# Stage 2 of a spectral kernel: one native fp32 product against three products of rounded high and low parts

## Chip, core and metric

The kernel runs on one core of a Trainium2 chip. The metric is device time in microseconds for one execution of the whole program; the time before is the median of three runs. The core has five engines that run side by side, each with its own queue that it works off in order: TensorE (matmuls; the profile lists its weight loads apart, as PEld), VectorE (DVE), ScalarE (ACT), GpSimd (POOL), and SyncE (SP), which here issues all DMAs.

## What is computed

The reference has two halves. The first filters every sequence in the frequency domain, the second is a gated feed-forward network with a convolution of three taps.

```python
X = np.fft.rfft(x, axis=1)                     # x: 8 x 3136 x 256
Yr = Xr @ w_r - Xi @ w_i + b_r
Yi = Xr @ w_i + Xi @ w_r + b_i
Y  = sign(Y) * max(|Y| - 0.01, 0)              # on Yr and Yi
y  = np.fft.irfft(Yr + 1j * Yi, n=3136, axis=1)
h  = max(y @ w_in, 0)                          # 256 -> 1024
c  = conv_w[0]*h[s-1] + conv_w[1]*h[s] + conv_w[2]*h[s+1]
out = (h * sigmoid(c)) @ w_out                 # 1024 -> 256
```

All inputs and the output are fp32, apart from the weights of the second half, which come as 64-bit numbers.

## The kernel before

The transform of length 3136 = 56 x 56 is done as two stages of products with tables. Stage 1 (`quads`, line 269) transforms over one factor and stores its result to a scratch tensor `sc1` in memory. Stage 2 (line 312) reads it back as `a2`, four values of u (a group, `UG` = 4) at a time, and multiplies with the table `t2`. The mix (line 340) applies the weights `w_r` and `w_i`. `shrink` (lines 352 to 354) cuts by 0.01. Stage 3 (line 363) is the first half of the inverse transform and stores to `sc2`. All this is the spectral part: eight batches of seven groups, 56 items, one item in each iteration of a loop of 60, of which stage 3 lags four iterations behind stage 2. Behind it comes the second half, with stage 4 (line 495), the products with `w_in` (line 520) and with `w_out` (line 548).

Two kinds of product are used. A native product takes fp32 operands as they are. A rounded product takes operands of the type fp32r, which holds fewer bits of the fraction; where these products are used (the mix, lines 520 and 548), each operand is split into a high part, the rounded value, and a low part, the rest, and three products (high x high, high x low, low x high) are summed in PSUM. Stages 1, 2, 3 and 4 use native products.

Inside the loop the order of the work is written out by hand (`manual_schedule`), and each engine's queue follows it. In iteration `it` it is:

1. SyncE loads `a2` of item it+2 (line 302, three buffers), in the first seven iterations the part of the table `inv1`, in the first six the part of the table `t2` that the next iteration needs (line 173), and x for stage 1 (line 261, three buffers).
2. TensorE does stage 3 of item it-4 and stage 1 of an item some eleven ahead. ScalarE and VectorE move their results out of PSUM (lines 369, 284, 285), and SyncE stores them.
3. From the fourth iteration on, VectorE does three steps of preparing the weights of the second half.
4. TensorE does stage 2 of item it: two tiles of 128 channels, four products each, 112 rows of `a2` as the stationary operand and 128 columns of `t2` as the moving one. For each tile ScalarE copies the imaginary half to `d` (line 315) and casts the result to the high part `fh` (line 316), and VectorE makes the difference `d` and the low part `fl` (lines 317 and 318).
5. `shrink` of item it-2: ScalarE makes `r` and `q`, GpSimd subtracts them.
6. `third` of item it: ScalarE casts `d` to a high part (line 323), GpSimd makes the low part (line 324).
7. The mix of item it-1: 36 rounded products of 256 columns, into three PSUM tiles. VectorE adds the bias into `p1` (line 344) and the sums into `v` (line 346).
8. In one of the early iterations (the fifth) a second stage 1 follows.

Stage 1, stage 2 and the mix share six PSUM banks (`psx`). Before the loop stands a head: the whole of stage 1 for the first batch, two more items, the weights of the mix (`load_mix`, whose raw tiles share two buffers), the first part of `t2` and the first two `a2`.

Of the kernel before, what the change touches and what calls it, by code (L numbers as in the profile page):

```python
# [9 lines left out]
F32 = mybir.dt.float32  # L10
F32R = mybir.dt.float32r
I32 = mybir.dt.int32
AF = mybir.ActivationFunctionType
ALU = mybir.AluOpType
# [3 lines left out]
B, S, D, FF = 8, 3136, 256, 1024  # L18
R = 56
U = 28  # L20
# [4 lines left out]
UG = 4  # L25
NG = U // UG
JC = 4
P = 128
# [96 lines left out]
def spectral_ffn_kernel(ctx: ExitStack, tc: tile.TileContext, x, w_r, w_i, b_r, b_i,  # L125
                        w_in, conv_w, w_out, fwd1, fwd2, inv1, inv2, out):
    nc = tc.nc
    K1, K2 = 2 * R, 2 * SP
# [13 lines left out]
    mlam, warm = small[:, 0:1], small[:, 1:2]  # L142


    with ExitStack() as ab:
        stg = ab.enter_context(tc.tile_pool(name="stg", bufs=1))
        wbp = ab.enter_context(tc.tile_pool(name="wbp", bufs=2))
        s1p = ab.enter_context(tc.tile_pool(name="s1p", bufs=2))
        c1 = ab.enter_context(tc.tile_pool(name="c1", bufs=1))
        a2p = ab.enter_context(tc.tile_pool(name="a2p", bufs=3))  # L150
        cmx = ab.enter_context(tc.tile_pool(name="cmx", bufs=1))
        DB, XRB, SL_ENG = 1, 3, nc.gpsimd
        psx = ab.enter_context(tc.tile_pool(name="psx", bufs=6, space=PSUM))
        psa = ab.enter_context(tc.tile_pool(name="psa", bufs=1, space=PSUM))

        f1 = c1.tile([P, P], F32, name="f1")[:, 0:SP]
        t2 = c1.tile([K1, U, K2], F32, name="t2")
        bias = cmx.tile([P, 2, D], F32, name="bias")
        cmx.tile([P, 96], F32, name="pad")
        wmix_hi = cmx.tile([P, NT, 3, D], F32R, name="wmix_hi")  # L160
        wmix_lo = cmx.tile([P, NT, 3, D], F32R, name="wmix_lo")
        inv1v = inv1.rearrange("p (u c m) -> p u c m", u=U // 2, c=2)
        fwd2v = fwd2.rearrange("p (u m) -> p u m", u=U)

        def split(dst_hi, dst_lo, src):
            nc.scalar.copy(dst_hi, src)
            nc.vector.tensor_tensor(dst_lo, src, dst_hi.bitcast(F32), op=ALU.subtract)
# [2 lines left out]
            nc.sync.dma_start(f1, fwd1)  # L170

        def load_t2(g):
            nc.sync.dma_start(t2[:, g * UG:(g + 1) * UG, :], fwd2v[:, g * UG:(g + 1) * UG, :])

        def load_mix():

            raw = [stg.tile([P, NT, D], F32, name=f"wm_raw{k}", tag="raw", bufs=2) for k in range(2)]
            for k in range(2):
                nc.sync.dma_start(raw[k], (w_r, w_i)[k].rearrange("(t p) e -> p t e", p=P))
            split(wmix_hi[:, :, 0, :], wmix_lo[:, :, 0, :], raw[1])  # L180
            for k, op in ((1, ALU.subtract), (2, ALU.add)):
                w = stg.tile([P, NT, D], F32, name="wm", tag="wm")
                nc.vector.tensor_tensor(w, raw[0], raw[1], op=op)
                split(wmix_hi[:, :, k, :], wmix_lo[:, :, k, :], w)

        def load_bias():

            for k in range(2):
                nc.sync.dma_start(bias[:, k, :], (b_r, b_i)[k].partition_broadcast(P))
# [66 lines left out]
        def load_x(pool, b, jc, **kw):  # L256

            xr = pool.tile([P, JC, D], F32, name="xr", **kw)
            xv = x[b].rearrange("(n h j) d -> h n j d", h=2, j=H)
            for h in range(2):  # L260
                ld = nc.sync.dma_start(xr[SP * h:SP * h + R], xv[h, :, jc * JC:(jc + 1) * JC, :])
            return xr, ld
# [37 lines left out]
        def load_a2(b, g):  # L300
            a2 = a2p.tile([K1, UG, D], F32, name="a2")
            ld = nc.sync.dma_start(a2, sc1[b].rearrange("(u q) j d -> (q j) u d", q=4)[:, g * UG:(g + 1) * UG, :])
            return a2, ld

        def stage2(g, a2):

            fh, fl = [wkf.tile([P, NT, 3, UG, SP], F32R, name=nm) for nm in ("fh", "fl")]
            d = wkf.tile([P, NT, UG, SP], F32, name="d", bufs=DB)
            for t in range(NT):
                ps = psx.tile([P, UG, 2, SP], F32, name="ps_s2", tag="bank")  # L310
                for k in range(UG):
                    nc.tensor.matmul(ps[:, k], a2[:, k, t * P:(t + 1) * P], t2[:, g * UG + k, :],  # L312
                                     start=(k == 0), stop=(k == UG - 1), skip_group_check=True)
                psv = ps.rearrange("p k c m -> p c k m")
                nc.scalar.copy(d[:, t], psv[:, 1])
                nc.scalar.copy(fh[:, t, 0:2], psv)
                nc.vector.tensor_tensor(d[:, t], psv[:, 0], d[:, t], op=ALU.subtract)
                nc.vector.tensor_tensor(fl[:, t, 0:2], psv, fh[:, t, 0:2].bitcast(F32), op=ALU.subtract)
            return fh, fl, d
# [7 lines left out]
        def mix(xs):  # L327


            fh, fl = xs  # L330
            ps = {c: psx.tile([K2, UG // 2, D], F32, name=f"ps_mx{c}", tag="bank") for c in (2, 0, 1)}
            for c in (2, 0, 1):
                q = (1, 2, 0)[c]
                for k in range(UG // 2):
                    mm = []
                    for t in range(NT):
                        a = [f[:, t, c, 2 * k:2 * k + 2, :] for f in (fh, fl)]
                        mm += [(a[0], wmix_hi[:, t, q, :]), (a[0], wmix_lo[:, t, q, :]), (a[1], wmix_hi[:, t, q, :])]
                    for n, (lt, rh) in enumerate(mm):
                        nc.tensor.matmul(ps[c][:, k, :], lt, rh, start=(n == 0), stop=(n == len(mm) - 1))  # L340
            p1 = wk.tile([K2, 2, UG // 2, D], F32, name="p1")
            v = wk.tile([K2, 2, UG // 2, D], F32, name="v")
            for c in range(2):
                nc.vector.tensor_tensor(p1[:, c], ps[2], bias[:, c:c + 1, :].to_broadcast([K2, UG // 2, D]), op=ALU.add)
            for c in range(2):
                nc.vector.tensor_tensor(v[:, c], ps[c], p1[:, c], op=ALU.add)
            return v

        def shrink(v):
            r = wk.tile([K2, 2, UG // 2, D], F32, name="r", bufs=3)  # L350
            q = wk.tile([K2, 2, UG // 2, D], F32, name="q", bufs=1)
            nc.scalar.activation(r, v, AF.Relu, bias=mlam)
            nc.scalar.activation(q, v, AF.Relu, bias=mlam, scale=-1.0)  # L353
            nc.gpsimd.tensor_tensor(r, r, q, op=ALU.subtract)  # L354
            return r

        def stage3_pe(g, r):
# [28 lines left out]
        n_it = len(items)  # L386
        WP0, LAST = 3, n_it - 6
        a2s = {}
        p1 = NG
        load_f1()  # L390
        with tc.tile_pool(name="hx", bufs=1, reuse_waits="tile") as hx:
            xh = []
            for p in range(NG):
                xr, ld = load_x(hx, 0, p, tag=f"hx{p}")
                xh.append(xr)
            with tc.issue_after(ld.ins):
                load_t2(0)
                load_mix()
                load_bias()
                st = stage1_head(xh)  # L400
        with tc.issue_after(st.ins):
# [4 lines left out]
            for i in range(2):  # L406
                a2s[i], ld = load_a2(*items[i])
        ab.enter_context(tc.issue_after(ld.ins))
        wkf, wk, cab, io = [ab.enter_context(tc.tile_pool(name=nm, bufs=n, reuse_waits="tile"))
                            for nm, n in (("wkf", 2), ("wk", 2), ("cab", 1), ("io", 2))]  # L410
        cab.tile([P, 56], F32, name="pad")
        i1 = cab.tile([K2, U // 2, 2, SP], F32, name="i1")
        wkf.tile([P, 56], F32, name="pad", bufs=1)
        wk.tile([P, 72], F32, name="pad", bufs=1)
# [9 lines left out]
                nx += 1  # L424

        with tc.manual_schedule():
            for it in range(n_it + LAG):
                if it + 2 < n_it:
                    a2s[it + 2], _ = load_a2(*items[it + 2])
                if it < NG:  # L430
                    load_inv1(it)
                    if it + 1 < NG:
                        load_t2(it + 1)
                fetch(XRB)
                if it >= LAG:
                    g3 = items[it - LAG]
                    ps3 = stage3_pe(g3[1], ss.pop(it - LAG))
                if p1 < n_it:
                    ps1 = stage1_pe(xq.pop(0))
                if it >= LAG:  # L440
                    stage3_out(*g3, ps3)
                if WP0 <= it < n_it:
                    next(background, None)
                if p1 < n_it:
                    stage1_out(*items[p1], ps1)
                    p1 += 1
                if WP0 <= it < n_it:
                    for _ in range(2):
                        next(background, None)
                if it < n_it:  # L450
                    xs[it] = stage2(items[it][1], a2s.pop(it))
                if 0 <= it - 2 < n_it:
                    ss[it - 2] = shrink(vs.pop(it - 2))
                if it < n_it:
                    xs[it] = third(xs[it])
                if 0 <= it - 1 < n_it:
                    vs[it - 1] = mix(xs.pop(it - 1))
                if p1 < n_it and p1 < min(it + AHEAD, NG + 2 + it + it // 2):
                    fetch(1)
                    ps1 = stage1_pe(xq.pop(0))  # L460
                    stage1_out(*items[p1], ps1)
                    p1 += 1
# [6 lines left out]
    wk, hp, io, y_b = pool("cwk"), pool("chp", 3), pool("cio"), pool("y_b")  # L469
# [143 lines left out]
```

## Time and profile before

| quantity | value |
|---|---|
| median of three runs | 1730.86 us (1730.43 to 1733.43) |
| the profiled execution | 1732.64 us |
| its span, first to last instruction | 1730.9 us |
| mean granted TensorE clock | 0.986 of full speed |
| spectral part | up to about 506 us |
| bytes moved by DMA | 163.77 MB, most in the spectral part |

The span is the profiled execution's time without the 1.7 us around it. A row of grouped instructions reads: line, engine, operation, the tiles written and read, the shape, the count, then after the bar the busy time in all, the mean of one in ns, and the idle time just before them with what ended it. A row of the chain in order of time reads: start, duration, engine and line or transfer, count. A row of the timeline reads: start, duration, engine, line, operation, tiles, shape, count, and in brackets the idle time before it. PEld is TensorE's load of the stationary operand, SPq the queue of SyncE. Tile names are shown without their digits: `t` is `t2`, `a` is `a2` or `a1`, `ps_s` stands for PSUM tiles of the stages.

### The profile page before, as it was taken

Reading aid. Unit: us, or ns where it says so; the run is one execution under the profiler, and the core shown is the slowest. Engines: PE = TensorE matmul, PEld = TensorE weight load, DVE = VectorE, ACT = ScalarE, POOL = GpSimd, SP = SyncE. Lnnn points to the kernel's source line nnn. Section 1 sums busy time; section 2 is a strip of 40 time slices with the busy share of each in tenths; the row PEclk is TensorE's granted clock in tenths of the full one; section 3 lists DMA queues with packets and bytes.
Section 4 is the critical chain, followed back from the end, with each engine's and each line's share of the span. In section 5 each row is a group of like instructions: output and inputs, shape, how many; then the busy total and the mean of one; then the engine's idle time right before and its main releaser. Section 6 shows DMA issues by size and latency. Waiting matters only on the chain.

```text
span 1730.9 us, 30421 instructions
## 1 busy us (share of the span) xinstructions
PE 1685.7 (97%) x12544; PEld 1556.3 (90%) x12544; DVE 1390.2 (80%) x1722; ACT 1197.5 (69%) x1589; POOL 209.9 (12%) x116
## 2 busy tenths in 40 slices
PE   4899999999998999999999999999999999999998
PEld 1688888888987999999999999999999999999998
DVE  2488888776546888888888888888888888888887
ACT  1477777677765777777777776776777677776776
POOL 0245445444440000000000000000000000000000
PEclk7899999999999999999999999999999999999999
DMA  8988888888432110111111011111101111100001
GB/s 222 250 259 244 235 248 248 217 225 237 139 101 72 54 43 23 43 54 44 43 54 44 22 43 55 43 43 55 43 22 47 51 43 44 43 22 23 22 22 43
DMA packets 115274, 163.77 MB, mean 95 GB/s; under 512 B 10680, under 2 KB 87728, under 8 KB 115136
## 3 DMA queue, kind: packets, MB, share of 16 engines
q1 hardware_dynamic: 115136, 161.83, 31.8%
q8 instruction: 99, 1.62, 0.4%
q14 instruction: 39, 0.32, 0.1%
HBM read 84.73 MB, written 77.07 MB: 93 GB/s over the span
## 4 chain that ended last, share of the span: by engine, by line
PE 95%; DMA 2%; DVE 1%; ACT 1%; issue 1%; SPq 1%; POOL 0%; ACTq 0%; DVEq 0%
PE acc L548 32%; PE ps_h L520 32%; PE ps_mx L340 14%; PE ps_s L312 7%; PE ps_s L495 6%; PE ps_s L363 3%; PE ps_s L269 3%; DMA xr<-in_x_dram 1%; DMA wm_raw<-in_w_i_dram 0%; SPq L274 0%; DVE yl L502 0%; ACT yh L501 0%; DMA sc<-ha 0%; DVE c L529 0%; DVE c L531 0%
## 5 line engine op out<-in xcount | busy, mean ns | idle before, releaser
L548 PE MATMUL acc<-wout,gh 128*128 128x256 f32 x3136 | 571.2, 281 | 0.0
L529 DVE SCALAR_TENSOR_TENSOR c<-h,cw,c 128x896 f32<-128x896 f32 x448 | 512.8, 1148 | 69.5 <-ACT c L527 66.5
L520 PE MATMUL ps_h<-yh,win 128*128 128x450 f32 x1792 | 550.3, 368 | 3.0 <-ACT yh L501 2.0
L548 PEld LDWEIGHTS acc<-wout,gh 128*128 128x128 f32 x3136 | 493.0, 188 | 6.1 <-ACT gh L534 0.3
L548 PE MATMUL acc<-wout,gl 128*128 128x256 f32 x1568 | 437.3, 280 | 0.4 <-DVE gl L535 0.4
L520 PEld LDWEIGHTS ps_h<-yh,win 128*128 128x128 f32 x1792 | 339.5, 189 | 29.3 <-ACT yh L501 2.2
L522 ACT ACTIVATE h<-ps_h 128x900 f32<-128x900 f32 x224 | 207.1, 924 | 197.5 <-PE ps_h L520 197.0
L520 PE MATMUL ps_h<-yl,win 128*128 128x450 f32 x896 | 329.8, 368 | 0.2 <-DVE yl L502 0.2
L548 PEld LDWEIGHTS acc<-wout,gl 128*128 128x128 f32 x1568 | 293.9, 188 | 1.2 <-DVE gl L535 0.6
L531 DVE TENSOR_TENSOR c<-h,c 128x896 f32<-128x896 f32 x224 | 243.7, 1088 | 40.9 <-ACT c L530 40.1
L535 DVE TENSOR_TENSOR gl<-c,gh 128x896 fp32r<-128x896 f32 x224 | 242.8, 1089 | 41.6 <-ACT gh L534 40.6
L534 ACT CAST gh<-c 128x896 fp32r<-128x896 f32 x224 | 210.7, 941 | 85.7 <-DVE c L531 85.7
L530 ACT ACTIVATE c<-c 128x896 f32<-128x896 f32 x224 | 212.5, 949 | 20.4 <-DVE c L529 18.3
L340 PE MATMUL ps_mx<-wmix_hi,fh 128*128 128x256 f32 x672 | 193.1, 287 | 0.0
L340 PE MATMUL ps_mx<-wmix_hi,fl 128*128 128x256 f32 x672 | 188.7, 281 | 1.7 <-POOL fl L324 1.7
L340 PE MATMUL ps_mx<-wmix_lo,fh 128*128 128x256 f32 x672 | 187.9, 280 | 0.0
L520 PEld LDWEIGHTS ps_h<-yl,win 128*128 128x128 f32 x896 | 169.4, 189 | 11.6 <-DVE yl L502 0.5
L527 ACT ACTIVATE c<-h,cw 128x896 f32<-128x896 f32 x168 | 175.9, 1047 | 1.8
L354 POOL TENSOR_TENSOR r<-r,q 128x1024 f32<-128x1024 f32 x56 | 133.5, 2384 | 235.8 <-ACT q L353 235.8
L312 PEld LDWEIGHTS ps_s<-t,a 112*128 112x128 f32 x896 | 106.8, 195 | 43.3 <-issue 39.2
L340 PEld LDWEIGHTS ps_mx<-wmix_hi,fl 128*128 128x128 f32 x672 | 126.6, 188 | 2.7 <-POOL fl L324 1.9
L340 PEld LDWEIGHTS ps_mx<-wmix_hi,fh 128*128 128x128 f32 x672 | 127.0, 189 | 0.4 <-issue 0.4
(77 smaller groups left out, 1715.1 us busy)
## 6 DMA issues: line engine op xcount, KB each, us to landing
xr<-in_x_dram SPq DMA_DIRECT2D x112, 224.0 KB
a<-sc SPq DMA_DIRECT2D x56, 448.0 KB
z<-sc SPq DMA_DIRECT2D x56, 448.0 KB
out_dram<-o SPq DMA_DIRECT2D x27, 896.0 KB
sc<-z SPq DMA_DIRECT2D x104, 224.0 KB
sc<-a SPq DMA_DIRECT2D x98, 224.0 KB
sc<-ha SPq DMA_DIRECT2D x14, 224.0 KB
win_bits<-in_moe_w_in_dram SPq DMA_DIRECT2D x4, 512.0 KB
```

The lines of the kernel that those rows point to most:

```text
L312: nc.tensor.matmul(ps[:, k], a2[:, k, t * P:(t + 1) * P], t2[:, g * UG + k, :], start=(k == 0), stop=(k == UG - 1), skip_group_check=True)
L340: nc.tensor.matmul(ps[c][:, k, :], lt, rh, start=(n == 0), stop=(n == len(mm) - 1))
L354: nc.gpsimd.tensor_tensor(r, r, q, op=ALU.subtract)
L520: nc.tensor.matmul(ps[:, a, 0:CH + 2], lt, rh, start=(n == 0), stop=(n == len(mm) - 1))
L522: nc.scalar.activation(h, ps[:, :, 0:CH + 2], AF.Relu)
L527: nc.scalar.mul(c, h[:, :, 0:CH], cw[:, 0, f:f + 1])
L529: nc.vector.scalar_tensor_tensor(c, h[:, :, k:k + CH], cw[:, k, f:f + 1], c, op0=ALU.mult, op1=ALU.add)
L530: nc.scalar.activation(c, c, AF.Sigmoid)
L531: nc.vector.tensor_tensor(c, h[:, :, 1:CH + 1], c, op=ALU.mult)
L534: nc.scalar.copy(gh, c)
L535: nc.vector.tensor_tensor(gl, c, gh.bitcast(F32), op=ALU.subtract)
L548: nc.tensor.matmul(acc[m // 2][:, m % 2, :], lt[:, sl], rh[:, f, :], start=(f == 0 and n == 0 and m % 2 == 0), stop=(f == NF - 1 and n == ...
```

## The change

Stage 2's native product becomes three rounded products. The table `t2` is kept as a high part `t2h` and a low part `t2l`; each part that is loaded goes to a raw tile first (in the two buffers of `load_mix`), ScalarE casts it to `t2h`, VectorE subtracts to get `t2l`. Each `a2` is split by ScalarE (cast to `ah`) and GpSimd (subtract to `al`), an iteration before stage 2 uses it. To make room, `a2` has two buffers in place of three, `p1` is dropped (the bias sum goes to `v` and is added up in place), and `q` is dropped (the second activation writes `v` in place, and GpSimd subtracts `v`). The splits of `t2` and of `a2` for item it+1 stand in iteration it ahead of stage 2 of item it; those for item 0 stand ahead of the loop.

```diff
-        a2p = ab.enter_context(tc.tile_pool(name="a2p", bufs=3))
+        a2p = ab.enter_context(tc.tile_pool(name="a2p", bufs=2))
...
-        t2 = c1.tile([K1, U, K2], F32, name="t2")
+        c1.tile([P, 96], F32, name="pad")
+        t2h = c1.tile([K1, U, K2], F32R, name="t2h")
+        t2l = c1.tile([K1, U, K2], F32R, name="t2l")
...
         def load_t2(g):
-            nc.sync.dma_start(t2[:, g * UG:(g + 1) * UG, :], fwd2v[:, g * UG:(g + 1) * UG, :])
+            raw = stg.tile([K1, UG, K2], F32, name="t2_raw", tag="raw", bufs=2)
+            nc.sync.dma_start(raw, fwd2v[:, g * UG:(g + 1) * UG, :])
+            return raw
+
+        def split_t2(g, raw):
+            sl = slice(g * UG, (g + 1) * UG)
+            split(t2h[:, sl, :], t2l[:, sl, :], raw)
...
+        def split_a2(a2):
+            ah = ahp.tile([K1, UG, D], F32R, name="ah")
+            nc.scalar.copy(ah, a2)
+            al = ahp.tile([K1, UG, D], F32R, name="al")
+            nc.gpsimd.tensor_tensor(al, a2, ah.bitcast(F32), op=ALU.subtract)
+            return ah, al
...
                 for k in range(UG):
-                    nc.tensor.matmul(ps[:, k], a2[:, k, t * P:(t + 1) * P], t2[:, g * UG + k, :],
-                                     start=(k == 0), stop=(k == UG - 1), skip_group_check=True)
+                    for n, (q, tab) in enumerate(((0, t2h), (0, t2l), (1, t2h))):
+                        nc.tensor.matmul(ps[:, k], a2[q][:, k, t * P:(t + 1) * P], tab[:, g * UG + k, :],
+                                         start=(k == 0 and n == 0), stop=(k == UG - 1 and n == 2), skip_group_check=True)
...
-            p1 = wk.tile([K2, 2, UG // 2, D], F32, name="p1")
...
-                nc.vector.tensor_tensor(p1[:, c], ps[2], bias[:, c:c + 1, :].to_broadcast([K2, UG // 2, D]), op=ALU.add)
+                nc.vector.tensor_tensor(v[:, c], ps[2], bias[:, c:c + 1, :].to_broadcast([K2, UG // 2, D]), op=ALU.add)
...
-                nc.vector.tensor_tensor(v[:, c], ps[c], p1[:, c], op=ALU.add)
+                nc.vector.tensor_tensor(v[:, c], ps[c], v[:, c], op=ALU.add)
...
-            q = wk.tile([K2, 2, UG // 2, D], F32, name="q", bufs=1)
...
-            nc.scalar.activation(q, v, AF.Relu, bias=mlam, scale=-1.0)
-            nc.gpsimd.tensor_tensor(r, r, q, op=ALU.subtract)
+            nc.scalar.activation(v, v, AF.Relu, bias=mlam, scale=-1.0)
+            nc.gpsimd.tensor_tensor(r, r, v, op=ALU.subtract)
...
+        ahp = ab.enter_context(tc.tile_pool(name="ahp", bufs=2, reuse_waits="tile"))
...
         with tc.manual_schedule():
+            split_t2(0, traw)
+            a2s[0] = split_a2(a2s[0])
             for it in range(n_it + LAG):
                 if it + 2 < n_it:
                     a2s[it + 2], _ = load_a2(*items[it + 2])
                 if it < NG:
                     load_inv1(it)
                     if it + 1 < NG:
-                        load_t2(it + 1)
+                        traw = load_t2(it + 1)
...
+                if it + 1 < NG:
+                    split_t2(it + 1, traw)
+                if it + 1 < n_it:
+                    a2s[it + 1] = split_a2(a2s[it + 1])
                 if it < n_it:
                     xs[it] = stage2(items[it][1], a2s.pop(it))
```

More of the change, by code (lines that the diff above doesn't have):

```diff
@@ L156, in spectral_ffn_kernel @@
         f1 = c1.tile([P, P], F32, name="f1")[:, 0:SP]
-        t2 = c1.tile([K1, U, K2], F32, name="t2")
+        c1.tile([P, 96], F32, name="pad")
+        t2h = c1.tile([K1, U, K2], F32R, name="t2h")
+        t2l = c1.tile([K1, U, K2], F32R, name="t2l")
         bias = cmx.tile([P, 2, D], F32, name="bias")
-        cmx.tile([P, 96], F32, name="pad")
         wmix_hi = cmx.tile([P, NT, 3, D], F32R, name="wmix_hi")
@@ L396, in spectral_ffn_kernel @@
             with tc.issue_after(ld.ins):
-                load_t2(0)
+                traw = load_t2(0)
                 load_mix()
```

## The prediction, made before the changed kernel was run

> **What bounds the kernel now.** I read the page first (engine shares, the chain by line), then the busy times by stretch, then the chain in order of time inside one iteration.
>
> ```profile
> span 1730.9 us, 30421 instructions
> PE 1685.7 (97%) x12544; PEld 1556.3 (90%) x12544; DVE 1390.2 (80%) x1722; ACT 1197.5 (69%) x1589; POOL 209.9 (12%) x116
> PE 95%; DMA 2%; DVE 1%; ACT 1%; issue 1%; SPq 1%; POOL 0%; ACTq 0%; DVEq 0%
> ```
> ```profile
> core 0: us, PE busy (x) PEld busy (x) DVE busy (x) ACT busy (x) POOL busy (x), PEclk, DMA share, GB/s
> 100.00:430.00 330.00, 329.04 (x3086) 279.87 (x3079) 260.69 (x466) 240.04 (x376) 152.98 (x81) 1.00 0.84 241
> ```
> ```profile
> 56.70 1.98 PE ps_s L312 x16
> ...
> 92.42 1.98 PE ps_s L312 x16
> 94.41 4.21 PE ps_mx L340 x36
> 98.61 1.02 PE ps_s L363 x16
> 99.64 0.86 PE ps_s L269 x8
> 100.50 1.98 PE ps_s L312 x16
> ```
>
> The chain is TensorE for 95%. In the spectral part TensorE works 329.04 of 330 us at full clock, so what its instructions need is what the time is. The chain shows one iteration: 1.98 us of stage 2, 4.21 of mix, 1.02 of stage 3, 0.86 of stage 1, together 8.08 (92.42 to 100.50). Every us added to stage 2 is added 56 times; the FFN behind it isn't touched. The other engines have room: of 8.08 us ScalarE works 5.9 (240.04/330), VectorE 6.4, GpSimd 3.7. The DMAs are the nearest neighbour, at 0.84.
>
> **The products.** What sets the 1.98 us is the question on which everything hangs.
>
> ```profile
> L340 PE MATMUL ps_mx<-wmix_hi,fh 128*128 128x256 f32 x672 | 193.1, 287 | 0.0
> L340 PEld LDWEIGHTS ps_mx<-wmix_hi,fh 128*128 128x128 f32 x672 | 127.0, 189 | 0.4 <-issue 0.4
> L340 PEld LDWEIGHTS ps_mx<-wmix_lo,fh 128*128 128x128 f32 x672 | 126.8, 189 | 0.0
> L312 PE MATMUL ps_s<-t,a 112*128 112x128 f32 x896 | 118.0, 286 | 0.0
> L495 PE MATMUL ps_s<-i,z 112*128 112x112 f32 x896 | 109.9, 277 | 4.6 <-DVE yl L483 3.1 <-DVE yl L502 1.5
> L312 PEld LDWEIGHTS ps_s<-t,a 112*128 112x128 f32 x896 | 106.8, 195 | 43.3 <-issue 39.2 <-ACT fh L323 1.6 <-ACT fh L316 1.4
> ```
> ```profile
> 253.82 1.86 PEld L312 LDWEIGHTS ps_s<-t,a 112*128 112x128 f32 x16 [0.81 <-issue]
> ...
> 506.33 3.65 PEld L495 LDWEIGHTS ps_s<-i,z 112*128 112x128 f32 x32 [0.39 <-DVE v L346]
> ```
>
> Line 312 issues 56 x 2 x 4 = 448 native products and shows 896 matmuls and 896 loads: a native product is two pairs of load and matmul. From the last rows, less one load of 0.19 us at the end, loads follow each other every (1.86 - 0.19)/15 = 111 ns in stage 2, and every (3.65 - 0.19)/31 = 112 ns in stage 4 (line 495). Stage 4 streams 112 columns, stage 2 streams 128: if streaming set the pace, stage 4 would be an eighth quicker. It isn't, and what both share is a load of 128 columns. So the load sets the pace, at 111 ns, and a shorter stream buys nothing. The mix (line 340) has the new type and 256 columns: 4.21/36 = 117 ns for one pair. Its load record is as long as the native one (189 against 195 ns), so the new type doesn't load faster.
>
> The Trainium skill, page "TensorE: Matmul & The Clock Gate", section "LDWEIGHTS (loading the stationary operand)", has a load take its number of columns over 1.2, 107 ns here; the trace's 111 agrees. The same page, "Back-to-back issue gap", states some 81 ns for pairs with 128 columns in a long stream; by that figure 24 pairs would be 1.94 us against 1.78 now (an estimate), and the two rows above speak against it.
>
> **Stage 2 after.** 16 pairs go, 4 x 2 x 3 = 24 come: 8 more at 111 ns is **+0.89 us** an iteration, **+50 us** in 56. Were all 24 to run at the mix's 117 ns, it is 24 x 0.117 - 16 x 0.111 = +1.03, or +58. I take 50: length of stream and of load are nearer to line 312 than to line 340. The ends are kept: 50 to 58 with the load as the bound.
>
> **The split of a2** (ScalarE cast, GpSimd subtract, one iteration ahead).
>
> ```profile
> L534 ACT CAST gh<-c 128x896 fp32r<-128x896 f32 x224 | 210.7, 941 | 85.7 <-DVE c L531 85.7
> L354 POOL TENSOR_TENSOR r<-r,q 128x1024 f32<-128x1024 f32 x56 | 133.5, 2384 | 235.8 <-ACT q L353 235.8
> ```
> ```profile
> 253.10 1.01 ACT L369 COPY z<-ps_s 128x1024 f32<-128x1024 f32 x1 [1.81 <-PE ps_s L363]
> 254.01 0.59 ACT L284 COPY a<-ps_s 128x512 f32<-128x512 f32 x1
> 255.07 0.37 ACT L315 COPY d<-ps_s 128x256 f32<-128x256 f32 x1 [0.47 <-PE ps_s L312]
> ...
> 258.75 0.62 ACT L323 CAST fh<-d 128x512 fp32r<-128x512 f32 x1
> ```
> ```profile
> 253.21 1.72 POOL L324 TENSOR_TENSOR fl<-d,fh 128x512 fp32r<-128x512 f32 x1
> ```
> ```profile
> 249.71 0.49 SPq L302 DMA_DIRECT2D a<-sc  x1
> ...
> 261.78 0.32 SPq L302 DMA_DIRECT2D a<-sc  x1
> ```
>
> The cast of 1024 columns is some 1.05 us (941 ns for 896, and 0.8 more per column), the subtract 2.38. ScalarE comes to 6.9 and GpSimd to 6.1 of now 8.97 us; neither is the bound. The cast sits ahead of stage 2's evacuations on ScalarE: from 254.6 to 255.65, where the engine idled 0.47 and TensorE is now busy longer. It pushes the rest (r, q, the third cast) by about 0.9 us at most: the third cast starts 4.93 us after stage 2 now, 5.85 then, when q has ended. From there GpSimd subtracts r (2.38) and makes the third low part (up to 1.72): done at 9.95. The next mix asks for it with its third pair, at 8.97 + 2.87 + 0.25 = 12.1. These 2.1 us are the cover, so the split costs **0**; what exceeds them lengthens the iteration.
>
> What shrinks is the lead of the loads of a2. With two buffers the load for it+2 waits for GpSimd to be done with a2 of it, and has to land for a cast in it+1. Two iterations hold cast, subtract, issue and landing: 1.05 + 2.38 + 0.5 + landing. With 10.49 us for a landing (quoted below) that is 14.4, under the 17.9 of two iterations: no cost. The load at 261.78 comes only 0.1 us before stage 2 (which starts 8.07 us after the 253.82 above), the one at 249.71 4.1 before. The first kind leaves 0.1 + 8.97 + 0.8 = 9.9 us, so the cast is late by 0.6, within the cover. I take **0**; the other end is a landing of 16 us (the load of 55.03 below is that of iteration 3, whose stage 2 starts at 71.15), where the ring gives (3.93 + 16.1)/2 = 10.0 us an iteration, +1.05 in each of some 42, **+44**.
>
> The smaller edits: p1 and q vanish into v, with the same additions and activations, at **0**: v is now held until GpSimd's subtract, which with two buffers ends well before the next-but-one mix writes it.
>
> **The split of t2** is the hidden part. In iterations 0 to 5 the table part for it+1 is loaded in iteration it, and ScalarE's cast of it stands in the same iteration ahead of the cast of a2 and of stage 2's evacuations. Now the load has a whole iteration.
>
> ```profile
> 1.21 3.70 DMA xr<-in_x_dram
> ...
> 12.68 7.11 DMA wm_raw<-in_w_i_dram
> ...
> 37.86 10.49 DMA xr<-in_x_dram
> ```
> ```profile
> 36.13 0.48 SPq L302
> ...
> 71.15 1.98 PE ps_s L312 x16
> ...
> 77.33 1.02 PE ps_s L363 x16
> ```
> ```profile
> 55.03 0.33 SPq L302 DMA_DIRECT2D a<-sc  x1
> 55.41 0.49 SPq L193 DMA_DIRECT2D i<-in_inv_dram  x1
> 55.96 0.45 SPq L173 DMA_DIRECT2D t<-in_fwd_dram  x1
> ```
> ```profile
> 19.81 0.62 ACT L166 CAST wmix_hi<-wm_raw 128x512 fp32r<-128x512 f32 x1 [8.41 <-DMA wm_raw<-in_w_i_dram]
> ```
>
> In SyncE's queue the order is a2, inv1, t2, x (55.03, 55.41, 55.96). The a2 load waits for the subtract of a2 two before, that subtract for its cast, and that cast is queued on ScalarE behind the t2 cast, which waits for the t2 of one iteration earlier. A **ring** closes: t2 lands, t2 cast 0.62, a2 cast 1.05, a2 subtract 2.38, issue of a2 and inv1 some 1.1, landing of the next t2. Landings in the trace: 3.7 (first load, nothing ahead), 7.1 (wm_raw, behind the x loads), 10.5 (x, in the fullest stretch). In the ring the queue empties between rounds and t2 has some 0.6 MB ahead of it; I take 7.1. One round is 0.62 + 1.05 + 2.38 + 1.1 + 7.1 = 12.25 us.
>
> The start: the first a2 are there by 49 (issued up to 36.13, ahead of the x that lands at 48.35). Cast and subtract end at 52.8; then a2, inv1 and t2 are issued, t2(1) lands at 61, the ScalarE and GpSimd work behind it ends at 65.2, and stage 2 of iteration 1 begins, where it began at 56.70. Five rounds later, at 126.5, stage 2 of iteration 6 begins. Stage 3 first runs in iteration 4 (77.33), so the rows of 92.42 and 100.50 are stage 2 of iterations 5 and 6, and the delay is 26. Of it 6 x 0.89 = 5 is counted in stage 2: +21. Once, in iteration 4, a second stage 1 at the end of the iteration puts its store in SyncE's queue ahead of the a2 load, behind all of ScalarE's work of that iteration: +5 by the casts and activations in between (r and q 1.1 each, the evacuations 2.2, the casts), so **+26**. With 3.7 us the round is 8.85 and the term +7, with 10.5 it is 15.65 and +46. VectorE's subtract of t2 (0.7 us, six times) lies beside the ring.
>
> **Sum.** The profiled execution took 1732.64: the span of 1730.9 and 1.7 around it. 1732.6 + 50 + 26 = 1809; the median of the runs, 1730.86, is 1.8 below that execution, so **1807**.
>
> **Rivals.**
> - *Two passes.* A rounded product of 128 columns has no row here; if it ran in two passes as a native one, 24 products are 48 pairs: 32 x 0.111 = +3.55 an iteration, +199; the ring then nearly hides (26 - 21 + 5 = 10). **1940**. For it: no rounded product in the trace has under 256 columns; against: the mix's 117 ns is one pass.
> - *Loads partly saved.* Two of three products share their weights; were that load skipped, 16 loads remain, stage 2 stays 1.78 and only the ring is left, +31: **1762**. Against: lines 340 and 312 show a load for every matmul, and line 340 too has two neighbours with the same weights. By the Trainium skill's 81 ns (the section named above) the time would be some 1770.
> - *Faster.* If the stream set the pace, 128 columns would take half of the mix's 117, 58 ns: 24 x 0.058 = 1.40, -0.38 an iteration, -21. With t2 landing in 3.7 us (+7, and 2 for the shorter iterations beside it) that gives **1719**. Below a pace of some 67 ns, where 24 products save 9 us, it decides; the equal pace of stage 4's shorter streams speaks against it.
> - *The a2 ring binds.* Landings of 16 us in the steady part: 1807 + 44 = **1851**. The 0.84 share of the DMAs speaks for it, the longer iteration, which spreads the same bytes over 8.97 us, against.
>
> **How the numbers follow.** Forecast 0.70, two passes 0.08, loads saved 0.06, faster 0.04, a2 ring 0.12. The forecast's own ends are 1788 (50 and 7) and 1835 (58 and 46). The range reaches from the loads-saved case to the a2 ring's: 1762 to 1851, which leaves out two passes, faster and what lies beyond the ends. A measurement of this kernel tells 0.2% (3.5 us) from no change: faster 0.04, same 0.02, slower 0.94.
>
> **What would show it.** 1344 matmuls of stage 2 with as many loads, loads 111 to 117 ns apart, stage 2 at some 2.9 us in the chain and an iteration of 9 us with TensorE still full: the first term. In the first 130 us ScalarE idle before a cast of t2 released by the t2 DMA, six times, and iterations of 12 us there: the ring. Loads 58 to 80 ns apart, or matmul records twice as many, would overturn the first term; idle TensorE between 130 and 430 us, with ScalarE waiting for a2, would show the a2 ring.

## The result: slower, 1.0343 of the time before

The changed kernel takes 1791.12 us (median of four runs, 1789.17 to 1793.31) against 1731.89 (four runs beside it): the ratio is 1.0343, interval 1.0328 to 1.0358. That is 59 us more; the forecast was 76 more, in a range of 31 to 120.

The page of the changed kernel, and its busy times behind the start, from 130 to 430 us (same columns; of before, 100 to 430 was shown):

```profile
span 1791.5 us, 31603 instructions
PE 1745.2 (97%) x12992; PEld 1613.0 (90%) x12992; DVE 1411.5 (79%) x1729; ACT 1257.7 (70%) x1652; POOL 347.6 (19%) x172
```
```profile
130.00:430.00 300.00, 299.25 (x2794) 258.95 (x2794) 230.96 (x396) 229.47 (x341) 209.24 (x100) 1.00 0.76 215
```

TensorE is the bound as before, 299.25 of 300 us; it has 448 more pairs of load and matmul (12992 against 12544), and the DMAs, with the same bytes over more time, fell from 0.84 to 0.76. In the list by line, stage 2 has three groups of 448, one load for each matmul; the chain in order of time shows one iteration:

```profile
L327 PE MATMUL ps_s<-t2h,ah 112*128 112x128 f32 x448 | 128.6, 287 | 0.0
L327 PEld LDWEIGHTS ps_s<-t2h,ah 112*128 112x128 f32 x448 | 88.3, 197 | 43.2 <-issue 36.7 <-ACT fh L338 2.4 <-ACT t2h L167 1.6
```
```profile
125.61 1.02 PE ps_s L376 x16
...
127.50 2.82 PE ps_s L327 x24
130.32 4.26 PE ps_mx L355 x36
134.58 1.02 PE ps_s L376 x16
```

From one stage 3 (125.61) to the next (134.58) it is 8.97 us, where it was 8.08. Stage 2 went from 1.98 to 2.82; the mix, 4.21 then and 4.26 now, and the rest stand. Single loads of the timeline, first and tenth of a group of 24, are (253.91 - 252.91)/9 = 111 ns apart:

```profile
252.91 0.19 PEld L327 LDWEIGHTS ps_s<-t2h,ah 112*128 112x128 f32 x1 [0.81 <-issue]
...
253.91 0.19 PEld L327 LDWEIGHTS ps_s<-t2h,ah 112*128 112x128 f32 x1
```

**Where the 60.6 us of span are.** Iteration 7 begins its stage 3 at 125.61; before, it began at 106.69, this row of its chain:

```profile
106.69 1.02 PE ps_s L363 x16
```

So 18.9 us are lost by then and 60.6 - 18.9 = 41.7 in the 49 items that follow, 0.85 each. The first seven items lose 6 at that rate. That leaves **48 us for the pairs** (56 x 0.85) and **13 us for the start**. A steady iteration is longer by 0.89, which would make 50; the mean is lower because the kernel before loses some 2 us of its own late in the loop, where its mix takes 4.41 and that of the changed kernel 4.25.

### The profile page after: what moved, and what is told of

It reads as the page before. It is cut to its first block, busy times and chain, and to the rows that moved or that the text cites. A ratio compares the mean times of both kernels' runs of the same rounds, so it can differ in the third digit from the quotient of the medians.

```text
span 1791.5 us, 31603 instructions
## 1 busy us (share of the span) xinstructions
PE 1745.2 (97%) x12992; PEld 1613.0 (90%) x12992; DVE 1411.5 (79%) x1729; ACT 1257.7 (70%) x1652; POOL 347.6 (19%) x172
## 4 chain that ended last, share of the span: by engine, by line
PE 94%; DMA 2%; ACT 1%; DVE 1%; SPq 1%; issue 1%; POOL 0%; ACTq 0%; POOLq 0%; DVEq 0%
PE acc L568 31%; PE ps_h L540 31%; PE ps_mx L355 13%; PE ps_s L327 9%; PE ps_s L515 6%; PE ps_s L376 3%; PE ps_s L276 2%; DMA t_raw<-in_fwd_dram 1%; DMA xr<-in_x_dram 1%; DMA a<-sc 0%; SPq L281 0%; DMA sc<-ha 0%; DMA sc<-a 0%; ACT ah L314 0%; DVE c L549 0%
## 5 line engine op out<-in xcount | busy, mean ns | idle before, releaser
L316 POOL TENSOR_TENSOR al<-a,ah 112x1024 fp32r<-112x1024 f32 x56 | 137.3, 2452 | 120.6 <-ACT ah L314 61.7
L367 POOL TENSOR_TENSOR r<-r,v 128x1024 f32<-128x1024 f32 x56 | 133.2, 2379 | 96.0 <-ACT v L366 94.7
```

The lines of the kernel that those rows point to most:

```text
L316: nc.gpsimd.tensor_tensor(al, a2, ah.bitcast(F32), op=ALU.subtract)
```

## Experiments

Theory A: eight more loads in each iteration are the steady cost, whatever their matmuls stream, and the splits are free there. The start had several candidates. Each ratio is to runs of the kernel before on the same chip, beside it.

| kernel | us | ratio to before, interval | steady iteration |
|---|---|---|---|
| before | 1731.9 to 1732.6 | 1 | 8.07 |
| changed | 1791.1 | 1.0343, 1.0328 to 1.0358 | 8.97 |
| e1 native product of the high parts | 1755.0 | 1.0128, 1.0108 to 1.0148 | 8.06 to 8.11 |
| e2 short streams | 1814.6 | 1.0474, 1.0447 to 1.0501 | 8.96, some 10.5 |
| e3 operands exchanged | 1747.3 | 1.0080, 1.0056 to 1.0103 | 7.70, some 8.1 to 8.6, one 13.8 |
| e4 t2 split late | 1796.0 | 1.0361, 1.0338 to 1.0385 | 8.97 |
| e5 three a2 buffers | 1786.9 | 1.0322, 1.0294 to 1.0349 | 8.97 |
| e7 a2 subtract twice | 1871.2 | 1.0782, 1.0735 to 1.0829 | 8.97, ten of 13.2 to 17.1 |
| e8 a2 cast twice | 1801.8 | 1.0396, 1.0364 to 1.0427 | 8.97 |
| e9 x loads first | 1789.2 | 1.0333, 1.0311 to 1.0356 | 8.97 |
| e10 subtract twice, weights behind the loop | 1864.3 (one run) | | 8.97 |
| e11 e5 and e9 together | 1786.6 | 1.0311, 1.0294 to 1.0328 | 8.97 |

### The products: e1, e2, e3

e1 keeps all but the products:

```diff
-                    for n, (q, tab) in enumerate(((0, t2h), (0, t2l), (1, t2h))):
-                        nc.tensor.matmul(ps[:, k], a2[q][:, k, t * P:(t + 1) * P], tab[:, g * UG + k, :], ...)
+                    nc.tensor.matmul(ps[:, k], a2[0][:, k, t * P:(t + 1) * P].bitcast(F32), t2h[:, g * UG + k, :].bitcast(F32), ...)
```

> All of the change stays (loads, splits, buffers, v in place), but stage 2 does one native product of the high parts again, 16 pairs of load and matmul instead of 24; the low parts are made and not used. Theory A (eight more loads an iteration are the steady cost, the splits cost nothing once the loop runs, the rest of the loss lies in the first 130 us): 1742 to 1746 us, which is the time before plus a start-up term of 10 to 14, iterations of 8.07 us in the steady part. Rival (the splits, the a2 buffers or the DMA lead cost in every iteration): over 1755, iterations over 8.2 us.

The chain of e1, one iteration:

```profile
252.82 1.02 PE ps_s L375 x16
...
254.70 1.98 PE ps_s L326 x16
...
260.88 1.02 PE ps_s L375 x16
```

Stage 2 is 1.98 us again and the iteration 8.06: with ScalarE's cast, GpSimd's subtract and two a2 buffers in every iteration, the steady loop runs as before. The time, 1755, missed its 1742 to 1746: its start costs 16.5 (stage 3 of iteration 7 at 123.17 in its chain, against 106.69), more than in the changed kernel (the start section comes back to it), and iterations of 8.11 and a longer end add some 5.

e2 leaves all 24 loads and shortens 16 of the streams. The low products of the imaginary half are left out:

```diff
                     for n, (q, tab) in enumerate(((0, t2h), (0, t2l), (1, t2h))):
-                        nc.tensor.matmul(ps[:, k], a2[q][:, k, t * P:(t + 1) * P], tab[:, g * UG + k, :], ...)
+                        w = P if n == 0 else SP
+                        nc.tensor.matmul(ps[:, k].rearrange("p c m -> p (c m)")[:, 0:w], a2[q][:, k, t * P:(t + 1) * P], tab[:, g * UG + k, 0:w], ...)
```

> The second and third product of each three stream 64 columns instead of 128 (the imaginary half gets no low products); the 24 loads an iteration stay. Theory A (the load of 128 columns sets the pace): 1791 within 4 us, loads still 111 to 112 ns apart. Rival (streamed columns set the pace, 256 instead of 384 for each three products): stage 2 shorter by up to a third, 0.9 us an iteration, some 1741.

Loads of the timeline (two, eleven steps apart), then the chain, then the busy times of the steady part, all of e2:

```profile
250.00 0.19 PEld L328 LDWEIGHTS ps_s<-t2h,ah 112*128 112x128 f32 x1
...
251.23 0.19 PEld L328 LDWEIGHTS ps_s<-t2h,al 112*128 112x128 f32 x1
```
```profile
269.45 4.28 PE ps_mx L356 x36
...
275.62 2.80 PE ps_s L328 x24
278.41 5.83 PE ps_mx L356 x36
```
```profile
130.00:430.00 300.00, 300.00 (x2680) 261.77 (x2679) 218.92 (x379) 218.79 (x326) 198.13 (x97) 0.95 0.74 207
```

Loads are (251.23 - 250.00)/11 = 112 ns apart, and stage 2 takes 2.80 us with a third of the streamed columns gone, 2.82 with all of them. The stream does not set the pace; the rival falls. The time none the less missed its place by 23 us, in the slow direction: the granted clock is 0.95 here instead of 1.00. In about every fourth iteration comes a stretch at half clock; here it falls on the mix, which was not edited and takes 5.83 us instead of 4.28. These are the iterations of 10.5.

e3 exchanges the roles: the table is loaded, a2 is streamed, 256 columns at a time. The result lies transposed, so it is not the reference's.

```diff
-                for k in range(UG):
+                for kk in range(2):
+                    k = 2 * t + kk
                     for n, (q, tab) in enumerate(((0, t2h), (0, t2l), (1, t2h))):
-                        nc.tensor.matmul(ps[:, k], a2[q][:, k, t * P:(t + 1) * P], tab[:, g * UG + k, :], ...)
+                        nc.tensor.matmul(ps.rearrange("p k c m -> p (k c m)")[:, kk * D:(kk + 1) * D], tab[:, g * UG + k, :], a2[q][:, k, :], ...)
```

> Stage 2 with the operands' roles exchanged: the tables are loaded (128 columns) and a2 is streamed (256 columns), so that the same three rounded products take 12 pairs an iteration instead of 24, with as many streamed columns in all; the result lies transposed and isn't the reference's. Theory A (pace of the load, until the stream is as long as the load): 12 pairs at 117 ns are 1.4 us instead of 2.7, -1.3 an iteration, near 1720; if another engine or the DMAs bind at 7.7 us, up to 1735. Rival (streamed columns or the number of multiplications set the pace): 1791, unchanged.

```profile
390.13 1.02 PE ps_s L377 x16
...
392.01 1.61 PE ps_s L328 x12
...
397.83 1.02 PE ps_s L377 x16
```

The chain of e3: the same three products, with as many streamed columns (12 x 256 = 24 x 128), take 1.61 us instead of 2.82, and the iteration is 7.70. Half the pairs, four sevenths of the time: it is the pairs that cost. That the load is what costs in a pair is argued and not shown: no run changes the width of the load. Stage 3, with loads of 64 columns, has its pairs 64 ns apart (1.02 us for 16), which speaks for the load, but its products are also smaller (64 x 64). The whole came to 1747, above the 1720 to 1735 expected: many iterations before 330 us take 8.1 to 8.6, one near 330 us takes 13.8, those at the end 7.6, and the start costs as in e1. What stretches those iterations is not shown.

### The start: e4, e5, e9, e11

The prediction put the start down to a ring through the cast of t2. The chain of the changed kernel from 40 us on:

```profile
44.81 2.35 POOL al L316
47.17 0.32 SPq L309
...
48.54 0.42 SPq L268
...
50.79 5.04 DMA xr<-in_x_dram
...
57.93 5.31 PE ps_s L327 x24
...
65.16 5.31 PE ps_s L327 x24
70.47 6.62 PE ps_mx L355 x36
...
103.81 0.33 SPq L309
...
104.72 5.54 DMA t_raw<-in_fwd_dram
```

Read from the top, the first column the start and the second the duration: the first subtract (44.81 to 47.16) releases the a2 load of iteration 0 (line 309), behind it in SyncE's queue come the x loads (line 268) for the stage 1 that stands ahead of stage 2 on TensorE, and stage 2 begins at 57.93 instead of 51.28. Then 24 pairs take 5.31 us and 36 take 6.62, twice the 2.82 and some one and a half times the 4.26 of later: half clock by their durations. (The clock record of this execution has 1.00 there; that of e5 has 0.50 over its first 24 pairs, which take the same 5.31 us.) Last, at 103.81, the ring that was predicted: a2, inv1 and t2 issued, 5.54 for t2 to land, the cast.

e4 moves the split of t2 behind `third`:

```diff
-                if it + 1 < NG:
-                    split_t2(it + 1, traw)
                 if it + 1 < n_it:
                     a2s[it + 1] = split_a2(a2s[it + 1])
...
                     xs[it] = third(xs[it])
+                if it + 1 < NG:
+                    split_t2(it + 1, traw)
```

> The split of t2 for the next iteration is moved behind stage 2, shrink and third of the current one; everything else as changed. Ring theory of the prediction (ScalarE's wait for t2 ahead of the a2 cast holds back the a2 subtract, and with it SyncE's next loads): the start-up term of some 13 us falls to 3 to 7, 1781 to 1786. Rival (the start is held by the a2 loads waiting for their buffer, with the x loads queued behind them, and by the half clock that follows): within 3 us of 1791.

It gained nothing: 1796 is above both expectations. Some 3 us of that lie in a stretch at half clock near 360 us (below). Its chain shows why this is no clean test of the ring: `t2l` now stands directly ahead of the stage 2 that needs it, and its subtract takes 1.67 us, 0.9 on the mean in the changed kernel. The ring is opened, and another wait is put in its place:

```profile
105.91 1.67 DVE t2l L168
...
107.62 3.55 PE ps_s L327 x23
```

That the ring exists, the chain of e1 shows, where TensorE has less to do and the landings of t2 come to lie on the chain:

```profile
82.38 3.92 DMA t_raw<-in_fwd_dram
...
92.25 4.62 DMA t_raw<-in_fwd_dram
...
102.93 4.92 DMA t_raw<-in_fwd_dram
```

Between the first two lie the casts, the a2 subtract and the issues, as predicted: a round of 9.9 us (9.6 in the chain of e9). In the second the a2 load waits for a stage 1 store, 10.7. A round is longer than an iteration of 8.97 by little and than one of 8.07 by more, which fits the start of 13 us in the changed kernel and of 16.5 in e1; that it is the whole of the difference is not shown.

e5 gives a2 its third buffer back (`bufs=3`), so that the first a2 load waits for nothing. e9 keeps two buffers and moves `fetch(XRB)` ahead of `load_a2`. e11 does both.

> As changed, with three buffers for a2 again. Theory B (the start is lost because the a2 load of iteration 0 now waits for the first subtract, and SyncE's queue, with the x that stage 1 ahead of stage 2 needs, waits behind it; the late start also keeps TensorE at half clock longer): stage 2 begins at some 52 us instead of 57.9, most of the 13 us come back, 1780 to 1785. Rival (the first casts, subtracts and the t2 loads are late by themselves): within 3 us of 1791.

> As changed (two buffers for a2), with the x loads of an iteration issued ahead of its a2, inv1 and t2 loads. Theory B (x behind the waiting a2 load is what delays the start): stage 2 begins earlier by 3 to 6 us, 1783 to 1788. Rival (not the order in SyncE's queue but the a2 split itself): within 3 us of 1791, or slower where a2 and t2 now land later.

> As changed, with three a2 buffers and the x loads issued first in each iteration. Theory B for the start (SyncE's queue behind the waiting a2 load): the two remedies meet the same cause, so together little more than each alone, 1780 to 1788; what stays over the time before is the pairs' 48 to 50 us and 2 to 6 at the start. Rival (two separate causes): the gains of e5 and e9 add up, 1776 or less.

The chain of e5:

```profile
40.38 9.55 DMA xr<-in_x_dram
...
52.88 5.31 PE ps_s L327 x24
...
116.94 1.02 PE ps_s L376 x16
```

Stage 2 begins at 52.88, as expected, and stage 3 of iteration 7 at 116.94 instead of 125.61: 8.7 of the 13 us are back. The time fell by 4 only (1786.9, beside the 1780 to 1785 expected), which the intervals do not separate from the changed kernel. In the profiled executions 3 us are lost again because an idle gap near 352 us, which the changed kernel has too, is followed here by a stretch at half clock: stage 2 takes 3.88 us there, and from stage 3 to stage 3 it is 13.9 us, where the changed kernel has 10.8.

```profile
351.86 0.75 issue
352.62 1.08 PE ps_s L276 x4
353.69 3.88 PE ps_s L327 x24
```

e9 begins stage 3 of iteration 7 at 118.03, 7.6 us earlier, and has the same loss near 355 us. By its time alone, 1789.2, its rival (within 3 us of 1791) would hold; the start in the trace is what speaks for theory B. Together (e11, 1786.6; stage 3 of iteration 7 at 117.35) they give no more than e5 alone: one cause, SyncE's queue behind an a2 load that waits for the first subtract. None of these four beats the kernel before; the best is 3.1% slower.

### The cover of the a2 split: e8, e7, e10

e8 issues ScalarE's cast of a2 twice (the first added line), e7 GpSimd's subtract (the second).

```diff
 def split_a2(a2):
             nc.scalar.copy(ah, a2)
+            nc.scalar.copy(ah, a2)
...
             nc.gpsimd.tensor_tensor(al, a2, ah.bitcast(F32), op=ALU.subtract)
+            nc.gpsimd.tensor_tensor(al, a2, ah.bitcast(F32), op=ALU.subtract)
```

> As changed, with ScalarE's cast of a2 issued twice. It adds 1.0 us ahead of everything that GpSimd waits for, less than the cover of 2.1. Cover theory: steady iterations stay at 8.97 us, 1791 within 5 (a few us more in the start at most). Rival (ScalarE's queue is on the path already): +0.5 us or more an iteration, over 1815.

> As changed, with GpSimd's subtract of a2 issued twice (the second writes the same values). The profile after leaves 2.1 us between the end of the third low part and the mix pair that reads it; the second subtract takes 2.4 to 2.6. Cover theory (the a2 split is free as long as GpSimd's row of work ends within those 2.1 us): the excess of 0.3 to 0.5 us shows in an iteration of 9.3 to 9.5 us, 1805 to 1820 in all. Rival (there is more cover than that, since GpSimd is busy for 8.7 of 8.97 us only): within 4 us of 1791.

e8: steady iterations stay at 8.97, so 1.0 us more ahead of GpSimd is free there. The time, 1802, is none the less outside the 5 us expected: the 10 us lie in the start (5) and in a stretch near 365 us (4). e7 is worse than either theory: ten iterations behind the start take 13.2 to 17.1 us, which is some 70 of the 80 us lost. VectorE and GpSimd in one of them, of 16.4 us (timelines), and its chain:

```profile
245.06 0.68 DVE L292 COPY a<-ps_s 128x512 f32<-128x512 f32 x1
...
248.24 4.94 DVE L223 TENSOR_SCALAR win_r<-win_bits 128x512 int32<-128x512 int32 x1
253.10 0.41 DVE L333 TENSOR_TENSOR d<-ps_s,d 128x256 f32<-128x256 f32 x1
```
```profile
245.36 2.40 POOL L316 TENSOR_TENSOR al<-a,ah 112x1024 fp32r<-112x1024 f32 x1 [0.52 <-ACT ah L314]
247.84 2.75 POOL L317 TENSOR_TENSOR al<-a,ah 112x1024 fp32r<-112x1024 f32 x1
250.55 2.35 POOL L368 TENSOR_TENSOR r<-r,v 128x1024 f32<-128x1024 f32 x1
```
```profile
250.71 1.02 PE ps_s L377 x16
...
252.59 1.62 issue
254.21 1.79 PE ps_s L276 x4
256.00 5.31 PE ps_s L328 x24
...
267.15 1.02 PE ps_s L377 x16
```

`win_r` on VectorE, 0.7 us on the mean in the changed kernel, lasts 4.94 here: it begins while GpSimd's second subtract runs, and ends (253.18) only when the one after it, to 252.90, is done too. The copy out of PSUM ahead of it (245.06) keeps its 0.68. It is not alone: line 222, which writes `win_m` from two inputs in SBUF, takes 3.6 us on the mean in e7 and 0.89 in the changed kernel (130 to 430 us), while `fl`, which reads PSUM, takes 0.68 in both. So an operation of VectorE that works on SBUF alone can stand still while GpSimd works, here through two of its instructions. The Trainium skill, "SBUF — State Buffer", section "SBUF: two separate sides", has the two engines share a pair of ports as an exclusive lock for whole instructions; of VectorE's operations it names those in a mode with two ports and those with two inputs in SBUF, and the loser waits. The trace agrees for line 222, 3.6 us against 0.89; whether `win_r`, with one input, falls under the first kind, no run shows. Behind `win_r` wait stage 2's differences, behind them PSUM banks, TensorE idles 1.62 us, and the next 24 pairs run at half clock (granted clock 0.50): 5.31 us instead of 2.82. With the stage 1 and the mix beside them, also slowed, a gap of 1.6 us costs this iteration 7.5.

e10 takes that preparation out of the loop, with the subtract still doubled:

```diff
-                if WP0 <= it < n_it:
-                    next(background, None)
...
-                if WP0 <= it < n_it:
-                    for _ in range(2):
-                        next(background, None)
...
+            for _ in background:
+                pass
```

> GpSimd's subtract of a2 twice, as in e7, and VectorE's preparation of the FFN weights taken out of the loop and done behind it, so that VectorE has hardly an operation left in the loop that reads and writes SBUF only (the whole time grows by the preparation behind the loop, some 60 to 90 us; the periods inside the loop are what is compared). Theory C (in e7 the two engines block each other on SBUF, VectorE's preparation waiting for whole GpSimd instructions, and TensorE's clock falls in the gaps that follow): iterations of 8.97 to 9.4 us between 130 and 430 us, no half clock there. Rival (GpSimd's chain is simply too long, by the excess over the cover of 2.1 us): iterations of 9.4 us and more, many of them 12 us as in e7.

```profile
130.00:430.00 300.00, 300.00 (x2810) 260.59 (x2810) 175.83 (x304) 228.98 (x337) 281.36 (x136) 1.00 0.68 208
```
```profile
251.20 1.02 PE ps_s L377 x16
...
260.17 1.02 PE ps_s L377 x16
```

The busy times and the chain of e10: GpSimd works 281 of 300 us, TensorE all 300 at full clock, an iteration is 8.97. The long iterations of e7 (16.4 us, not the 12 that this expectation gives them) come from the two engines blocking each other, not from the length of GpSimd's chain. The time of e10, from a single run, has the preparation as work of its own behind the loop and is not compared.

## Why the prediction was right, and where it was not

- **The pace of a pair** carried it. It was read from two native stages with streams of 128 and 112 columns and the same spacing, and said to hold for the rounded type. Spacing 111 ns, 24 pairs in 2.82 us (2.9 forecast), iteration 8.97 (8.97 forecast), 48 us in all (50 forecast). e2 shows the independence from the stream, e3 the dependence on the number of pairs; that the load is what sets it stays an argument. The rivals with two passes, with a saved load and with the stream as the bound are out: 448 loads for 448 matmuls in each group, one record for each product.
- **The start** was the mis-sized term: +26 forecast, 13 measured. Its entry came out right by luck (stage 2 of iteration 1 at 65.2 forecast, 65.16 measured). The forecast let the first subtract end at 52.8 and t2 land at 61; the subtract ended at 47.16, and the a2 split for iteration 1 was done at 60.3. What held stage 2 were the x loads behind the waiting a2 load, for which the sum has no term and which e5 and e9 show to be about two thirds of what is lost, and TensorE's own 24 pairs at half clock. The five rounds of 12.25 us failed too. The ring is there, but a round is 9.6 to 9.9 us where it can be seen (e9, e1), since t2 mostly landed in 3.9 to 5.5 us where 7.1 was taken (8.0 once, in e5), and in most rounds of the changed kernel TensorE's own work, at half clock at first, was as long. ScalarE idled before a cast of t2 four times in the loop (1.15 to 5.12 us), not six. (The lower end of the term, +7 for a landing of 3.7 us, comes to some 6 by the prediction's own steps; no reading hangs on it.) From iteration 1 to 5 the iterations were 12.95, 8.09, 9.29 and 8.97 us; only the next two, 10.44 and 12.59, show the ring beside a store that had to land. How much of these two is t2's cast and how much the store is left open: e4, meant to show it, brought a wait of its own.
- **The a2 split at 0** holds (e1: 8.06 to 8.11 with all of it). Its reason was too narrow: e10 has 2.4 us more on GpSimd, above the stated 2.1 of cover, at no cost to the iteration, with GpSimd still idle for 19 of 300 us. The price named for more than the cover, the excess itself, was too small: e7 lost 80 us, by a mechanism that the prediction did not name.
- **The a2 ring** did not bind: TensorE idle for 0.75 of the 300 us from 130 to 430, and the DMAs fell to 0.76.
- The edits of `p1` and `q` cost nothing that shows in the steady iteration, as forecast.

## What to carry to other kernels

Count pairs of load and matmul, and compare two stages with different streams: where the spacing is equal, the stream does not set it, and three short rounded products cost three pairs against a native product's two. In this kernel split operands shortened the steady iteration only after exchanging them (e3, 7.70 against 8.07), and even then the whole was 0.8% slower. When a buffer is taken away to make room, look at which queue its next load blocks, and what stands behind it.

## What was not expected of the hardware

- With streams of 64 columns TensorE's clock fell to half for short stretches although TensorE was busy in 300.00 of 300 us (e2, granted clock 0.95 on the mean and 0.71 over the mix that took 5.83 us against 4.28). It lengthens 14 iterations by 1.55 us each, some 22 us in all. The Trainium skill, "TensorE: Matmul & The Clock Gate", section "What's actually happening", lets the clock follow how busy the array has been, and names idle windows as what lowers it; here no idle time was seen, and the measurement decides. That the array counts as less busy with short streams is an inference.
- Short gaps are dear, but not always: 1.62 us of waiting in e7 was followed by 24 pairs in 5.31 us, 0.75 us near 352 us in e5 by 3.88 (e4, e9 and e11 have such a stretch there too, granted clock 0.73 to 0.76 over 12 to 14 us, and iterations of 13.9 to 14.0). The same kind of gap in the profiled execution of the changed kernel (0.75 us at 360 us) was followed by 2.83. What decides between the two is not shown:

```profile
360.53 0.75 issue
...
362.36 2.83 PE ps_s L327 x24
```
